# Reordering the second quad in the first batch: q turned before k, scores and exps by head pairs between AV units

## The chip, the cores and the metric

The kernel runs on one core of a Trainium2 chip. The metric is the device time of one execution in microseconds (us), median over several runs. Each ratio, with its 95% interval, is against runs of the kernel before. Kernels are compared only within the same rounds.

## The reference, cut to what matters

Eight batches of eight heads: attention of 512 local positions in a window of 32 to each side, plus 32 global positions that see and are seen by all. A gated feed-forward layer on the result (512 to 2048 to 512).

```python
k_all = np.concatenate([k_g, k_l], axis=2)
s_g   = scale * np.matmul(q_g, k_all.transpose(0, 1, 3, 2))      # global rows see everything
out_g = np.matmul(sm(s_g), v_all)
s_ll  = np.where(np.abs(pos[:, None] - pos[None, :]) <= 32, scale * q_l @ k_l.T, -1e9)
s_l   = np.concatenate([scale * q_l @ k_g.T, s_ll], axis=-1)
out_l = np.matmul(sm(s_l), np.concatenate([v_g, v_l], axis=2))
...
h = x @ w_in
return (h * sigmoid(1.702 * h)) @ w_out
```

## The kernel before: the parts concerned

Four heads make a quad; the first batch is quads `a` and `c`. A quad's scores come in two rounds, each a tile of four PSUM banks, one bank a head. `psS` holds one such tile; a ring of four one-bank tiles, `psP`, serves everything else (K's scores `kb`, the AV units `ov`, and so on).

```python
psS = ctx.enter_context(tc.tile_pool(name="psS", bufs=1, space=bass.MemoryType.PSUM))
psP = ctx.enter_context(tc.tile_pool(name="psP", bufs=4, space=bass.MemoryType.PSUM))
... # class Quad (cut)
    def B(self, rnd, split=False):        # the window's bias, added on TensorE: 8 matmuls of 128x128
    def S(self, rnd, ...):                # scores: 2 chunks x 2 halves of d, 4 heads in 4 row groups
        for c in (2 * rnd, 2 * rnd + 1):
            ...                           # rows and columns of the chunk (cut)
            for e in range(2):
                for j in range(4):
                    p = slice(32 * j, 32 * j + 32)
                    nc.tensor.matmul(ps[j][:, off : off + n], lhsT=self.k[p, 128 * c : 128 * c + 128, e],
                                     rhs=self.q[p, lo:hi, r0 : r0 + nr, e], ...)
    def X(self, rnd):                     # exps: all four banks in one ACTIVATE
        ...                               # the branch for scores in four separate tiles (cut)
        nc.scalar.activation(e[:, :, :RW], self.ps[:, :, :RW], AF.Exp, scale=scale)
        if rnd == self.gr:                # the global rows' exp
            nc.scalar.activation(e[:, 2, RW:], self.ps[:, 2, RW : RW + 32], AF.Exp, scale=scale)
```

`Tk` and `Tq` turn (transpose) k and q on VectorE, `ext` adds q's extra rows; `gg` and `K` are small 32x32 matmuls of the global part, `XK` is K's exp; `ekU(u)` and `U(u)` are the AV unit u, exps times values (0 is the softmax's sum, 1 and 2 the values); `R` and `XL` normalise, and `XL` writes what the first hidden matmuls read. The schedule of the first batch:

```python
a.X(1)
c.Tk(); c.ext(); c.Tq()
cast_g32("v", rvg)
c.B(0); a.K(); a.XK()
c.S(0, added=True); c.gg(); c.X(0)
a.eg(); c.K(); c.XK()
a.ekU(0); a.U(0); a.R()
a.ekU(1); a.U(1); a.XL(0)
c.B(1); c.S(1, added=True); c.X(1)
a.ekU(2); a.U(2); a.XL(1); a.Gm()
... # then c's three AV units, c.R, c.XL and the first hidden matmuls, which wait for c.XL
```

The softmax here doesn't subtract the row's maximum and nothing guards it: scores larger than these inputs give would overflow.

Of the kernel before, what the change touches and what calls it, by code (L numbers as in the profile page):

```python
# [15 lines left out]
AF = mybir.ActivationFunctionType  # L16
# [4 lines left out]
def kernel(  # L21
# [12 lines left out]
    nc = tc.nc  # L34

    B, H, Sl, D = q_l.shape
    Sg = q_g.shape[2]
    S = Sg + Sl
    n_tokens = B * S
    d_model = H * D  # L40
    d_ff = moe_w_in.shape[1]
    assert (B, H, Sl, Sg, D) == (8, 8, 512, 32, 64)
    W = 32
    scale = 1.0 / (D ** 0.5)
# [6 lines left out]
    RW = 428  # L51
# [62 lines left out]
    def cast_g32(name, t):  # L114
        nc.vector.tensor_copy(t[:, 0:2, :D], g32[name])
# [67 lines left out]
    def near(t, c):  # L183
        lo = 0 if c else 2
        return t[:, :, lo : lo + WIN[c][1]]
# [44 lines left out]
    def pbank(name):  # L230
        return psP.tile([128, 512], F32, name=name, tag="p")

    class Quad:
# [37 lines left out]
                    qgT[:, self.Q, : n * nr].rearrange("p (t r) -> p t r", t=n))  # L271


        def B(self, rnd, split=False):
            self.bk[rnd] = [pbank("s") for _ in range(4)] if split else self.spt(rnd)
            ps = self.bk[rnd] if split else [self.bk[rnd][:, j, :] for j in range(4)]
            for c in (2 * rnd, 2 * rnd + 1):
                w = (40, 200, 36, 228)[c]
                for j in range(4):
                    nc.tensor.matmul(ps[j][:, w : w + 16 * WIN[c][1]], lhsT=ident, rhs=near(bias, c),  # L280
                                     start=(c == 2 * rnd), stop=False, skip_group_check=True)

        def S(self, rnd, split=False, added=False, part=None):
            if not added:
                self.bk[rnd] = self.spt(rnd)
            ps = self.bk[rnd] if split else [self.bk[rnd][:, j, :] for j in range(4)]
            for c in (2 * rnd, 2 * rnd + 1):
                off = (0, 200, 0, 228)[c]
                r0, nr = WIN[c]
                t0, t1 = ((0, 20), (4, 23), (1, 20), (4, 24))[c]  # L290
                lo, hi = ((t0, t1) if part is None else (12, t1) if part else (t0, 12))
                off += (lo - t0) * nr
                n = (hi - lo) * nr
                for e in range(2):
                    for j in range(4):
                        p = slice(32 * j, 32 * j + 32)
                        nc.tensor.matmul(  # L297
                            ps[j][:, off : off + n],
                            lhsT=self.k[p, 128 * c : 128 * c + 128, e],
                            rhs=self.q[p, lo:hi, r0 : r0 + nr, e],  # L300
                            start=(e == 0 and not added), stop=(e == 1), skip_group_check=True,
                        )
            if not part:
                self.E[rnd] = att.tile([128, 4, RW + 32], BF16, name="e%d" % rnd)
            if split:
                self.gk(ps[2][:, RW : RW + 32], self.qg)
            self.ps = self.bk[rnd]
# [9 lines left out]
                                     rhs=rv[:, :, ee] if len(rv.shape) == 3 else rv[:, :, :, ee],  # L317
                                     start=(ee == 0), stop=(ee == 1), skip_group_check=True)

        def X(self, rnd):  # L320
            e = self.E[rnd]
            if isinstance(self.ps, list):
                for j in range(4):
                    n = RW + 32 if j == 2 else RW
                    nc.scalar.activation(e[:, j, :n], self.ps[j][:, :n], AF.Exp, scale=scale)
                return
            nc.scalar.activation(e[:, :, :RW], self.ps[:, :, :RW], AF.Exp, scale=scale)  # L327
            if rnd == self.gr:
                nc.scalar.activation(e[:, 2, RW:], self.ps[:, 2, RW : RW + 32], AF.Exp, scale=scale)

        def M(self, rnd):
            at = 36 if rnd else 40
            e = self.E[rnd][:, :, at : at + LW]
            nc.vector.tensor_mul(e, e, mask[:, rnd : rnd + 1, :].to_broadcast([128, 4, LW]))  # L334
# [161 lines left out]
    def o_out(i, tci, op):  # L496
        ob = moe.tile([128, d_model], F32, name="ob", bufs=6)
        last = i == B and tci == B // 4 - 1
        for lo, hi in ((0, 320), (320, 512)) if last else ((0, 512),):
            if last:  # L500
                op = pbank("op")
                for fc in range(FC):
                    nc.tensor.matmul(op[:, lo:hi], lhsT=gTs[i][:, fc, tci * 128 : tci * 128 + 128],  # L503
                                     rhs=w_out_sb[:, fc, lo:hi], start=(fc == 0), stop=(fc == FC - 1))
            nc.scalar.activation(ob[:, lo:hi], op[:, lo:hi], AF.Copy, scale=0.5)  # L505
            for j in range(4):
                eng = nc.scalar if last and j % 2 else nc.sync
                if i < B:
                    rows = out[i * S + Sg : (i + 1) * S, :].rearrange("(r t) m -> t r m", t=16)[4 * tci + j]
                else:  # L510
                    r = (4 * tci + j) * S
                    rows = out[r : r + Sg, :]
                eng.dma_start(out=rows[:, lo:hi], in_=ob[32 * j : 32 * j + 32, lo:hi])
# [8 lines left out]
    a, c = Quad(0), Quad(1)  # L522

    def zero(n, ps):
        for _ in range(n):
            nc.tensor.matmul(ps, lhsT=warm[:, 0:128], rhs=warm, start=False, stop=False, skip_group_check=True)
# [25 lines left out]
    a.S(1, split=True, added=True)  # L552
    zero(3, a.bk[1][3])
    a.X(1)
    c.Tk()
    c.ext()
    c.Tq()
    cast_g32("v", rvg)
    c.B(0)
    a.K()  # L560
    a.XK()
    c.S(0, added=True)
    c.gg()
    c.X(0)
    a.eg()
    c.K()
    c.XK()
    a.ekU(0)
    a.U(0)
    a.R()  # L570
    a.ekU(1)
    a.U(1)
    a.XL(0)
    c.B(1)
    c.S(1, added=True)
    c.X(1)
    a.ekU(2)
    a.U(2)
    a.XL(1)
# [42 lines left out]
    a, c = nq[1]  # L622
# [49 lines left out]
    a, c = nq[2]  # L672
# [83 lines left out]
    for i in range(1, B):  # L756
        if i > 1:
            for fc in range(FC):
                h_step(i, fc)
        if i + 1 < B:  # L760
            phase_o(i)
# [36 lines left out]
```

## Time and profile before

| | before |
|---|---|
| time, median of 3 runs | 311.05 us (310.76 to 311.09) |
| span of the profiled run | 309.3 us |
| TensorE / VectorE / ScalarE busy | 97% / 68% / 54% |
| first scores of `c` start | 12.20 us |
| AV of `c` starts | 18.05 us |
| first matmul that waits for `c.XL` | 21.19 us |

How to read it: TensorE is the bound, and from 21.19 us on it has hardly an idle moment. Up to there it waits on loads, turns and exps. So a change in this stretch is worth what it moves the moment at 21.19, if nothing behind takes it back. The lines are in the prediction.

### The profile page before, as it was taken

The page shows a single profiled execution, that of the slowest core. Times are in us where ns is not written, and L with a number is a line of the kernel's source. Part 1 is how long each engine was busy: PE and PEld are TensorE (multiplying, and loading weights), DVE is VectorE, ACT ScalarE, POOL GpSimd, SP SyncE. Part 2 cuts the span into 40 slices and gives each one's busy share as a digit, 9 for nine tenths or more (in the row PEclk, how much of TensorE's full clock was granted, in tenths as well). Part 3 has the DMA queues.
Part 4 walks back from the last instruction along what each step waited for, and adds up shares of the span by engine and source line. Part 5 has one row for each costly group of instructions (what it writes and reads, how often), then busy time and mean ns, then how long its engine had stood idle before and what let it go on. Part 6 is the DMA issues. An engine that isn't in the chain of part 4 may idle for free.

```text
span 309.3 us, 7765 instructions
## 1 busy us (share of the span) xinstructions
PE 299.2 (97%) x3230; PEld 149.3 (48%) x3265; DVE 211.0 (68%) x446; ACT 167.6 (54%) x251; POOL 54.1 (18%) x86
## 2 busy tenths in 40 slices
PE   7899999999999999999999999999999999999994
PEld 6544445444454455444454455445454454446653
DVE  6668857978957876776867876776777855573320
ACT  4728475475546735565556645565456651673421
POOL 8542754630050001400050002100000000000000
PEclk9999999999999999999999999999999999999999
DMA  7999999999289013951199013901120012201122
GB/s 193 176 209 206 201 138 217 213 184 100 61 79 192 5 36 72 131 107 30 45 95 173 8 37 71 101 0 36 36 61 10 2 44 46 51 0 35 35 68 69
DMA packets 53859, 27.60 MB, mean 89 GB/s; under 512 B 42432, under 2 KB 43712, under 8 KB 53824
## 3 DMA queue, kind: packets, MB, share of 16 engines
q0 software_dynamic: 45696, 16.95, 48.2%
q1 hardware_dynamic: 7648, 9.51, 12.6%
q10 hardware_dynamic: 480, 0.66, 0.7%
q8 instruction: 25, 0.41, 0.6%
q14 instruction: 10, 0.08, 0.1%
HBM read 35.13 MB, written 8.91 MB: 142 GB/s over the span
## 4 chain that ended last, share of the span: by engine, by line
PE 88%; DVE 4%; ACT 2%; DMA 2%; issue 1%; POOL 1%; ACTq 0%; POOLq 0%
PE op L491 35%; PE hp L466 35%; PE s L297 6%; PE ov L397 4%; PE ov L374 3%; DMA rk<-in_k_l_dram 2%; ACT e L327 1%; DVE xL L430 1%; PE s L316 1%; PE op L503 1%; DVE gT L474 1%; PE s L466 1%; PE s L415 1%; ACT th L473 1%; PE kb L316 1%
## 5 line engine op out<-in xcount | busy, mean ns | idle before, releaser
L491 PE MATMUL op<-w_out_sb,gT 128*128 128x512 bf16 x504 | 120.0, 380 | 1.7 <-issue 0.5
L474 DVE SCALAR_TENSOR_TENSOR gT<-th,hp 128x512 bf16<-128x512 f32 (+1 forms) x140 | 91.1, 656 | 41.8 <-ACT th L473 40.5
L466 PE MATMUL hp<-xL,w_in_sb 128*128 128x512 bf16 x487 | 108.4, 379 | 0.7
L473 ACT ACTIVATE th<-hp 128x512 f32<-128x512 f32 (+1 forms) x140 | 79.8, 573 | 42.9 <-PE hp L466 39.4
L466 PEld LDWEIGHTS <-w_in_sb 128*128 128x128 bf16 x576 | 56.1, 98 | 65.0 <-issue 1.3
L491 PEld LDWEIGHTS <-gT 128*128 128x128 bf16 x528 | 49.3, 98 | 56.4 <-issue 3.5
L327 ACT ACTIVATE e<-s 128x1712 bf16<-128x1712 f32 x31 | 49.5, 1597 | 15.8 <-PE s L415 8.9
L505 ACT ACTIVATE ob<-op 128x512 f32<-128x512 f32 (+2 forms) x35 | 20.5, 585 | 60.3 <-PE op L491 57.7
L89 POOL DMA_DIRECT2D v<-in_v_l_dram x24 | 18.7, 786 | 115.9 <-PE s L415 111.0
L421 DVE STREAM_TRANSPOSE sT<-ov 128x512 f32<-128x512 f32 x15 | 10.8, 717 | 29.1 <-PE ov L397 29.1
L334 DVE TENSOR_TENSOR e<-e,mask 128x1408 bf16<-128x1408 bf16 x28 | 24.4, 871 | 6.5 <-ACT e L327 6.5
L297 PE MATMUL s<-q,kT 32*128 32x228 bf16 (+5 forms) x528 | 21.1, 280 | 0.9 <-DVE q L259 0.7
L430 DVE TENSOR_TENSOR xL<-ov,rs 128x512 bf16<-128x512 f32 x30 | 19.4, 686 | 1.8 <-PE ov L397 0.5
L297 PEld LDWEIGHTS <-kT 32*128 32x128 bf16 x528 | 11.1, 95 | 14.8 <-issue 9.4
L255 DVE STREAM_TRANSPOSE kT<-rk 128x512 f32<-128x512 f32 (+1 forms) x17 | 16.9, 993 | 1.4 <-DMA rk<-in_k_l_dram 1.3
L362 ACT ACTIVATE ek<-kb 128x512 bf16<-128x512 f32 x16 | 9.6, 601 | 9.5 <-PE kb L316 9.5
L397 PE MATMUL ov<-e,v 128*32 128x160 bf16 (+1 forms) x480 | 12.1, 239 | 0.0
L425 DVE STREAM_TRANSPOSE rs<-rT 128x512 f32<-128x512 f32 x16 | 11.4, 711 | 0.5
L259 DVE STREAM_TRANSPOSE q<-rq 128x512 f32<-128x512 f32 (+1 forms) x17 | 10.7, 634 | 0.0
L397 PEld LDWEIGHTS <-v 128*32 128x32 bf16 x512 | 10.0, 97 | 0.9 <-issue 0.9
L316 PE MATMUL kb<-q,kgT 32*32 32x512 bf16 x128 | 10.0, 386 | 0.0
L466 PE MATMUL hp<-xG,w_in_sb 128*128 128x256 bf16 x64 | 9.6, 273 | 0.1
(78 smaller groups left out, 165.9 us busy)
## 6 DMA issues: line engine op xcount, KB each, us to landing
out_dram<-ob SPq DMA_DIRECT2D x132, 64.0 KB, 1.7
v<-in_v_l_dram POOLq DMA_DIRECT2D x32, 128.0 KB, 6.5
rq<-in_q_l_dram POOLq DMA_DIRECT2D x6, 512.0 KB, 8.5
rk<-in_k_l_dram POOLq DMA_DIRECT2D x6, 512.0 KB, 10.4
w_out_sb<-in_moe_w_out_dram POOLq DMA_DIRECT2D x4, 512.0 KB, 11.3
w_in_sb<-in_moe_w_in_dram POOLq DMA_DIRECT2D x4, 256.0 KB, 10.2
w_in_sb<-in_moe_w_in_dram POOLq DMA_DIRECT2D x2, 512.0 KB, 12.5
rq<-in_q_l_dram POOLq DMA_DIRECT2D x3, 256.0 KB, 7.9
```

Of the source, the lines that this page charges most:

```text
L89: nc.gpsimd.dma_start(out=vtiles[b % 2][p, s, :, :, :D], in_=vf[b, g][:, hs])
L255: nc.vector.transpose(self.kT.rearrange("p (r t) -> p t r", t=16)[:, lo:hi], loaded[self.b][0][:, self.u].bitcast(F32)[:, 32 * lo : 32 * hi])
L297: nc.tensor.matmul(ps[j][:, off : off + n], lhsT=self.k[p, 128 * c : 128 * c + 128, e], rhs=self.q[p, lo:hi, r0 : r0 + nr, e], start=(e == ...
L327: nc.scalar.activation(e[:, :, :RW], self.ps[:, :, :RW], AF.Exp, scale=scale)
L334: nc.vector.tensor_mul(e, e, mask[:, rnd : rnd + 1, :].to_broadcast([128, 4, LW]))
L397: nc.tensor.matmul(ov[32 * j : 32 * j + 32, :].rearrange("p (t r) -> p t r", t=16)[:, :, r0 : r0 + nr], lhsT=lv, rhs=self.E[c // 2][:, j, ...
L430: nc.vector.tensor_mul(self.x[:, 2 * self.u + h, :], self.st[1 + h], self.st["rs"])
L466: nc.tensor.matmul(hp[:, : width(i)], lhsT=w_in_c[:, fc // 8, kc, fc % 8 // 2, :, fc % 2], rhs=(xL[i] if i < B else xG)[:, kc, :], start=( ...
L473: nc.scalar.activation(th[:, :n], hp[:, :n], AF.Tanh, scale=0.851)
L474: nc.vector.scalar_tensor_tensor(gTs[i][:, fc, :n], in0=th[:, :n], scalar=1.0, in1=hp[:, :n], op0=ALU.add, op1=ALU.mult)
L491: nc.tensor.matmul(op, lhsT=gTs[i][:, fc, tci * 128 : tci * 128 + 128], rhs=w_out_sb[:, fc, :], start=(first and fc == 4 * f4), stop=(fc = ...
L505: nc.scalar.activation(ob[:, lo:hi], op[:, lo:hi], AF.Copy, scale=0.5)
```

## The change

The intent: q lands before k, so turn it in that idle time; do the scores and exps of `c` two heads at a time, so that the second scores of a pair can go into the banks that the first pair's exp has freed; and fill TensorE's waits with the AV units of `a`. The core of the diff:

```diff
-        def S(self, rnd, split=False, added=False, part=None):
+        def S(self, rnd, split=False, added=False, part=None, js=range(4)):
...
-                    for j in range(4):
+                    for j in js:
...
+            if js is not None:
+                nc.scalar.activation(e[:, js, :RW], self.ps[:, js, :RW], AF.Exp, scale=scale)
+                return
...
-    c.Tk()
+    c.Tq()
     c.ext()
-    c.Tq()
+    c.Tk()
...
-    c.X(0)
+    c.X(0, slice(0, 2))
+    c.X(0, slice(2, 4))
+    c.Xg()
     a.eg()
-    c.K()
-    c.XK()
     a.ekU(0)
     a.U(0)
     a.R()
+    c.K()
+    c.B(1, js=(0, 1))
+    c.S(1, added=True, js=(0, 1))
+    c.X(1, slice(0, 2))
+    c.XK()
     a.ekU(1)
     a.U(1)
     a.XL(0)
-    c.B(1)
-    c.S(1, added=True)
-    c.X(1)
+    c.B(1, js=(2, 3))
+    c.S(1, added=True, js=(2, 3))
+    c.X(1, slice(2, 4))
```

More of the change, by code (lines that the diff above doesn't have):

```diff
@@ L271, in ext, with B @@
                     qgT[:, self.Q, : n * nr].rearrange("p (t r) -> p t r", t=n))
-        def B(self, rnd, split=False):
-            self.bk[rnd] = [pbank("s") for _ in range(4)] if split else self.spt(rnd)
+        def B(self, rnd, split=False, js=range(4)):
+            self.bk[rnd] = [pbank("s") for _ in range(4)] if split else self.pt if len(js) < 4 else self.spt(rnd)
             ps = self.bk[rnd] if split else [self.bk[rnd][:, j, :] for j in range(4)]
@@ L294, in S @@
                 for e in range(2):
-                    for j in range(4):
+                    for j in js:
                         p = slice(32 * j, 32 * j + 32)
@@ L302, in S @@
                         )
-            if not part:
+            if not part and 0 in js:
                 self.E[rnd] = att.tile([128, 4, RW + 32], BF16, name="e%d" % rnd)
@@ L318, in gk, with X @@
                                      start=(ee == 0), stop=(ee == 1), skip_group_check=True)
-        def X(self, rnd):
+        def X(self, rnd, js=None):
             e = self.E[rnd]
+            if js is not None:
+                nc.scalar.activation(e[:, js, :RW], self.ps[:, js, :RW], AF.Exp, scale=scale)
+                return
             if isinstance(self.ps, list):
@@ L329, in X, with Xg @@
                 nc.scalar.activation(e[:, 2, RW:], self.ps[:, 2, RW : RW + 32], AF.Exp, scale=scale)
+        def Xg(self):
+            nc.scalar.activation(self.E[self.gr][:, 2, RW:], self.ps[:, 2, RW : RW + 32], AF.Exp, scale=scale)
         def M(self, rnd):
@@ L554 @@
     a.X(1)
+    c.Tq()
+    c.ext()
     c.Tk()
-    c.ext()
-    c.Tq()
     cast_g32("v", rvg)
```

## The prediction

> **What bounds the kernel now.** I read the page first, then the chain of waits over the first 50 us, then the timeline engine by engine from 8 to 24 us, down to windows of tens of ns.
>
> ```profile
> PE 299.2 (97%) x3230; PEld 149.3 (48%) x3265; DVE 211.0 (68%) x446; ACT 167.6 (54%) x251; POOL 54.1 (18%) x86
> ...
> PE 88%; DVE 4%; ACT 2%; DMA 2%; issue 1%; POOL 1%; ACTq 0%; POOLq 0%
> ```
>
> TensorE (PE) is busy for 97% of the span and is 88% of the chain that ended last: whatever moves PE's dense part earlier or later moves the end. The change touches only the first batch, before that dense part begins at 21.19 us (from 21.19 to 33.40 us PE is busy 12.16 of 12.21). So the question is when the matmul that starts at 21.19 us will start. The chain of waits up to it:
>
> ```profile
> 3.02 7.18 DMA rk<-in_k_l_dram
> ...
> 11.13 0.40 DVE q L269 x4
> 11.53 0.63 DVE q L259
> ...
> 12.20 0.67 PE s L297 x16
> ...
> 13.08 1.60 ACT e L327
> ...
> 14.81 0.77 PE s L280 x8
> ...
> 16.98 0.70 DVE xL L430
> ...
> 17.72 0.40 PE ov L374 x4
> 18.12 0.45 PE ov L397 x15
> ```
>
> The second quad's k lands at 10.20, is turned on VectorE (DVE), then come q's extra rows and q, then the scores (12.20), their exp (13.08), the second bias and scores (14.81), and then not those scores' exp but the first quad's last normalisation (16.98): the second quad's third AV bank is the buffer which that frees at 17.67. At 18.05 its AV units start, and its R, XL and the wait for them lead to 21.19, 3.14 us later. The timeline of PE and ScalarE (ACT):
>
> ```profile
> 12.85 0.39 PE L374 MATMUL ov<-ek,ones 32*32 32x512 bf16 x4
> 12.86 0.62 PE L316 MATMUL kb<-q,kgT 32*32 32x512 bf16 x8
> 13.41 0.49 PE L397 MATMUL ov<-e,ones 128*32 128x160 bf16 x16
> ...
> 12.02 0.64 ACT L362 ACTIVATE ek<-kb 128x512 bf16<-128x512 f32 x1
> 13.08 1.60 ACT L327 ACTIVATE e<-s 128x1712 bf16<-128x1712 f32 x1 [0.42 <-PE s L316]
> ...
> 16.23 1.60 ACT L327 ACTIVATE e<-s 128x1712 bf16<-128x1712 f32 x1 [0.98 <-PE s L297]
> ```
>
> From 12.70 to 18.05 PE is nearly full already (1.95 of 2.10 us, then 3.14 of 3.25): there is little idle time for a better order to fill.
>
> **What the Trainium skill says.** (1) "TensorE: Matmul & The Clock Gate", Part 3: matmuls in different row groups run concurrently, starting about 4 ns apart. The trace agrees: the four head matmuls of a scores step start within 12 ns (12.200 to 12.212) and the next step 105 to 133 ns later. So two heads need the same four steps as four heads. (2) "TensorEngine Tiling (Array Packing)", Key Properties: changing the tiling mode drains the array. The trace agrees: the last scores matmul starts at 12.576 and the next of another tile shape at 12.796; its 228 columns[...] are an estimated 95 ns, which leaves 125 ns; after K (last start 13.10, 213 ns of columns) U starts at 13.41, which leaves 97 ns. I take 0.1 us a change. (3) "ScalarE: Activation LUTs", What ACT_TABLE_LOAD costs: an ACTIVATE takes 186 ns and 0.833 ns an element, and neighbours overlap by some 93 ns. For 1712 elements that is 1612 ns, the trace has 1597; the two halves should start 0.78 us apart. (4) "PSUM — Partial Sum Buffer", PSUM bank collisions: guard PSUM by bank and quadrant. This program's own waits look coarser, by tile:
>
> ```profile
> 52.75 0.49 PE L397 MATMUL s<-e,ones 128*32 128x160 bf16 x16
> 53.07 0.78 PE L397 MATMUL s<-e,v 128*32 128x160 bf16 x32
> ...
> 53.90 0.72 DVE L421 STREAM_TRANSPOSE sT<-s 128x512 f32<-128x512 f32 x1 [0.33 <-PE s L397]
> ```
>
> The transpose reads only the bank of the first unit, whose matmuls end by 53.24, but it starts at 53.90, after the 53.85 end of the third unit, which is in another bank of the same four-bank tile. Also the tanh of banks 0 and 1 waits at 23.11 for the matmul into bank 3. In one-bank tiles units release one by one (sT starts at 18.59, while the other units still run).
>
> **The change part by part.**
>
> *q before k.* The second quad's q lands at 8.55, k at 10.20; DVE is idle from 8.91 to 10.22. Turning q (0.70) and its rows (0.40) fits in there, so the scores need only kT (10.22 + 1.05 = 11.27). But PE is then at the bias and K: K's last matmul starts at 11.46, with 0.21 and 0.10 of drain the array is free at 11.77. Scores start 11.77 instead of 12.20: 0.43 earned, not the 1.1 of DVE work. Of that AV gets less: gg ends issuing at 12.42, then ekU(0) needs ek, whose exp on ACT runs until 12.66 as before. ekU(0) starts at 12.71, U(0) at 13.03 (was 13.41).
>
> *K moved behind U(0).* Before, K and ekU(0) shared the array: both within 12.85 to 13.41, 0.56 us. Apart they take 0.32 (13.83 to 14.15 for another ekU) and about 0.56 (11.21 to 11.77): 0.31 more of PE. U(0) to K takes 0.42, so K 13.45, and PE is ready for the bias at 14.01.
>
> *Second scores by pairs.* Bias: 8 matmuls stay 8, 0.70 becomes 0.39 twice (one more drain). Scores: 0.60 from 15.51 to 16.11 for four steps; each pair needs four steps, so 0.56 twice: +0.52. All this on PE, in front of U(2).
>
> *The exps.* Only bank reuse can pay: the new bias goes into the banks of the first scores, no new tile. If waits go by bank it starts at 14.01. If by tile, as above, it must wait for the whole first exp: first half from 12.65, second 13.43, the global one 14.21 to 14.40, bias at 14.45, 0.44 later.
>
> **Sum, waits by tile.** Bias 14.45, scores 14.84, ekU(1) 15.40, U(1) 15.72; exp of pair one, 0.72 after its scores' start as at present, 15.56 to 16.46. PE is ready for the second bias at 16.14 but waits for that exp until 16.51. Scores 16.90, ekU(2) 17.46, U(2) 17.78. In the kernel before, U(2) starts at 16.43 and the second quad's AV at 18.05, 1.62 later, by XL(1) and the bank it frees; that stays, for exp of pair two ends at about 18.5 and does not bind. So AV starts at 19.40: **1.35 us late**.
>
> **Sum, waits by bank.** Bias 14.01, scores 14.41, ekU(1) 14.96, U(1) 15.28, bias 15.70, scores 16.10, ekU(2) 16.65, U(2) 16.97, AV 18.59: **0.54 us late**. In both, the second exp ends at 17.7 to 18.5, hardly before or even after the 17.83 of today, so the pairs earn nothing.
>
> Behind it all stays in order, and nothing absorbs the shift: the weights for the eighth hidden chunk land at 25.89 and are used at 27.2, the last output weights at 39.00 and are used at 41.3, and the third k at 41.87, used by scores at 47.06. A later start only widens these. So the delay goes through to the end, one for one.
>
> **Rivals.** (a) Faster by some 0.4 to 0.6 us: the scores' earlier start goes through. For it: 0.43 at 12.20, and the chain runs through q and the first exp. Against: PE is almost full from there on, and the change adds about 0.9 us of PE time in front of U(2) (0.31 + 0.08 + 0.52). It would need pairs at half the cost of four heads, U(2) at about 16.0: 310.5. (b) Waits by bank, only PE time added: 311.6. (c) Waits by tile, 312.4. (d) Hidden anyway: the second exp ended at 17.83, only 0.2 us before AV, and if the bank freed by XL(1) stopped binding, AV could start about when PE gets there: within 0.2 of 311.05. Against: the order of buffers at that point is unchanged, XL(1) still needs U(2). (e) A transfer becomes the bound: only if PE ran over 1.2 us early, which nothing here gives.
>
> **Range and chances.** I give (c) about 0.7, (b) 0.2, (a) and (d) 0.1. That puts the middle at 312.2. Runs of the kernel before differ by 0.3, another chip may add as much. Range 311.1 to 312.9. Two per cent is 6.2 us, over four times the largest shift here: a verdict of "same" is nearly sure.
>
> **What would show it.** The q transpose at about 8.8 to 9.5, and the first score of the second quad near 11.8, show step one. K alone for 0.56 after U(0) shows the lost sharing. Eight scores in about 0.56 rather than 0.30 show that pairs don't halve. The bias with a wait on the global exp (tile) or none (bank) tells (c) from (b). The first matmul that now waits for XL at 21.19 should be at about 22.5 (c) or 21.7 (b), and the rest of the trace displaced by as much. The prediction is wrong if pairs cost 0.3 each, if PE can run K beside U, or if the later part takes back the delay, to be seen if the shift at 21.19 is not the shift of the span.

## The result, and the profile after

The changed kernel took 311.45 us (median of 6, 311.14 to 311.94) against 310.99 for the kernel before (6 runs); the ratio is 1.0014, interval 1.0001 to 1.0027. A second set gave 311.71 against 310.90, ratio 1.0026 (1.0013 to 1.0040). A ratio is the mean time of one kernel's fast runs over that of the other's of the same rounds, so it is not quite the ratio of the medians. The verdict is "same" at 2%, with a small loss that both intervals hold clear of zero, the first barely: 0.14 to 0.26% of 311 us, 0.4 to 0.8 us.

First the page's lines of the engines and of the chain, in the changed kernel:

```profile
PE 299.6 (97%) x3230; PEld 149.1 (48%) x3265; DVE 211.3 (68%) x446; ACT 167.8 (54%) x253; POOL 54.1 (17%) x86
...
PE 90%; ACT 3%; DVE 3%; DMA 1%; issue 1%; ACTq 0%
```

As many matmuls as before and two ACTIVATEs more. The chain of waits (start, length, what; `issue` is time in which the engine waited for nothing that the profile shows) shows what changed:

```profile
1.28 4.37 DMA k<-in_k_l_dram
...
9.67 1.71 ACT e L328 x4
11.38 0.49 ACT ek L368
11.87 1.65 ACT e L323 x2
13.52 0.10 ACT e L335
13.62 0.04 issue
13.66 0.46 PE s L280 x4
14.12 0.61 PE s L297 x8
14.73 0.02 issue
14.75 0.89 ACT e L323
15.64 0.04 issue
15.69 0.46 PE s L280 x4
16.15 0.59 PE s L297 x8
```

Read it against the chain before. There the DMA at its head was the load of `c`'s k, then VectorE's turns. Here it is the load of `a`'s k, then `a`'s exps, K's exp, both halves of `c`'s first exp and the global one (13.52), and only then the bias of the first pair (13.66), its scores, its exp, and again only after that exp the bias of the other pair (15.69). The pairs go through strictly one after the other. TensorE's timeline has the two waits behind it, and what eight score matmuls cost (start, length, what; a bracket gives the engine's idle time just before and what ended it):

```profile
13.66 0.46 PE L280 MATMUL s<-bias,ident 128*128 128x192 bf16 x4 [0.36 <-ACT e L335]
14.05 0.66 PE L297 MATMUL s<-q,kT 32*128 32x228 bf16 x8
14.64 0.40 PE L380 MATMUL ov<-ek,rvg 32*32 32x512 bf16 x4
14.96 0.49 PE L403 MATMUL ov<-e,v 128*32 128x160 bf16 x16
15.69 0.46 PE L280 MATMUL s<-bias,ident 128*128 128x192 bf16 x4 [0.23 <-ACT e L323]
```

The bias of heads 0 and 1 waits for the global exp, which reads bank 2; the bias of heads 2 and 3 waits for an exp of banks 0 and 1. Neither uses the other's bank. And the eight scores occupy the array from 14.05 to 14.64, 0.59 us, where sixteen took 0.60 (15.51 to 16.11) in the kernel before:

```profile
15.51 0.67 PE L297 MATMUL s<-q,kT 32*128 32x228 bf16 x16
16.11 0.40 PE L374 MATMUL ov<-ek,rvg 32*32 32x512 bf16 x4
```

The moments of several traces, for all that follows. X is the start of `a`'s first exp, L the landing of `c`'s k, S the start of `c`'s first scores, AV that of its AV units.

| trace | X | L | S | AV | S to AV |
|---|---|---|---|---|---|
| before | 8.87 | 10.20 | 12.20 | 18.05 | 5.85 |
| changed | 8.08 | 9.80 | 10.98 | 18.61 | 7.63 |
| changed, second trace | 9.22 | 10.64 | 12.13 | 19.76 | 7.63 |
| changed, k first | 8.36 | 10.91 | 12.91 | 20.54 | 7.63 |
| changed, two tiles | 8.16 | 10.19 | 11.31 | 18.00 | 6.69 |
| q first, K late | 8.87 | 10.30 | 11.78 | 17.70 | 5.92 |
| q first alone | 8.27 | 10.01 | 11.17 | 17.02 | 5.85 |
| copies on ScalarE | 8.43 | 10.77 | 12.77 | 18.62 | 5.85 |

Clock times can't be compared across rows, since X and L differ by 1.1 us from run to run whatever the kernel; differences within a row can, and they repeat to 0.01 us. With k first, S is L + 2.00 in all three rows. With q first it is X + 2.91, or L + 1.1 to 1.2 where k is late.

### The profile page after: what moved, and what is told of

Same layout as the page of the kernel before. It is cut to its first block, busy times and chain, and to the rows that moved or that the text cites. A ratio compares the mean times of both kernels' runs of the same rounds, so it can differ in the third digit from the quotient of the medians.

```text
span 309.4 us, 7768 instructions
## 1 busy us (share of the span) xinstructions
PE 299.6 (97%) x3230; PEld 149.1 (48%) x3265; DVE 211.3 (68%) x446; ACT 167.8 (54%) x253; POOL 54.1 (17%) x86
## 4 chain that ended last, share of the span: by engine, by line
PE 90%; ACT 3%; DVE 3%; DMA 1%; issue 1%; ACTq 0%
PE op L497 37%; PE hp L472 36%; PE s L297 6%; PE ov L403 4%; PE ov L380 3%; DMA k<-in_k_l_dram 1%; ACT e L330 1%; DVE xL L436 1%; ACT e L323 1%; PE op L509 1%; PE s L316 1%; PE s L472 1%; PE s L421 1%; ACT e L328 1%; PE kb L316 1%
## 5 line engine op out<-in xcount | busy, mean ns | idle before, releaser
L330 ACT ACTIVATE e<-s 128x1712 bf16<-128x1712 f32 x29 | 46.3, 1597 | 14.0 <-PE s L421 8.9
```

## The experiments

Theory: q first earns, and the pairs lose, by two terms: matmul time (a pair costs what four heads cost) and waits that fall on the whole four-bank tile. Rivals: the pairs lose by matmul time alone; K's new place loses; q first is hidden.

**q first alone.** The only edit to the kernel before:

```diff
-    c.Tk()
+    c.Tq()
     c.ext()
-    c.Tq()
+    c.Tk()
```

> Kernel before with only the first part of the change: the second quad's q turned ahead of its k. Theory (q first earns, the rest of the change loses): from the first quad's first exp to the first matmul that waits for the second quad's XL it took 12.32 us before (8.87 to 21.19) and 13.67 in the changed kernel (8.08 to 21.75); here it takes 11.9, and the time is 310.4 to 310.7, 0.1 to 0.2% below before. Rival (q first is hidden, because the array is held by the first quad's K anyway): 12.3 and 311.0.

Measured: 310.03 us against 310.94, ratio 0.9985 (0.9962 to 1.0007; one run of six at 312.28 widens it). The stretch from X took about 11.96 us: the first hidden matmuls waited for a load of weights and then ran until 20.23, worked out as 18.715 plus seven spacings of 0.216, since one record is missing.

> q first alone once more, beside the version above: its first time was 310.03 with an interval that reached no difference. Theory: 310.0 to 310.4 and a ratio of 0.997 to 0.999; the first scores to AV take 5.85 us as before and start 1.1 to 1.2 us after k lands or 2.9 us after the first quad's exp starts, whichever is later. Rival: no difference from before, 310.9.

Measured: 310.00 against 310.95, ratio 0.9991 (0.9959 to 1.0023; one run of six at 313.51). S to AV was 5.84, S came 2.91 after X. The medians are 0.9 us below before both times, but these two intervals reach no difference; what secures the gain is the trace (S no longer 2.00 after L) and the comparisons below with k first again, K late and the last version.

**The changed kernel with k first again.** The same edit undone:

> The changed kernel with k turned first again. Theory: the order of the turns is a gain of 0.4 us or more inside a net loss, so the stretch takes 14.0 to 14.3 us and the time is 311.8 to 312.2. Rival (the turns do nothing): 13.7 and 311.45.

Measured: 312.38 us, ratio 1.0046 (1.0033 to 1.0059). So the turns' order is a gain inside the net loss. The direction met the theory; both figures went beyond it, the time by 0.2 us and the stretch, 15.32 us, by a whole one, because in that trace k landed late (10.91), and with k first all waits for that. S to AV is 7.63 as in the changed kernel, so the loss sits entirely behind S.

**q first and K late**, scores and exps whole and in their old places:

```diff
     a.eg()
-    c.K()
-    c.XK()
     a.ekU(0)
     a.U(0)
     a.R()
+    c.K()
+    c.XK()
```

> q first, and K and its exp moved behind the first quad's U(0) and R; scores and exps whole and in their old places. Theory: K apart costs PE 0.3 to 0.4 us which nothing hides: the stretch takes 12.2 to 12.3 us, the time about 310.9. Rival (only the pairs lose): as q_first, 11.9 and 310.6.

Measured: 310.39 us, ratio 0.998 (0.9968 to 0.9992), stretch 11.97, S to AV 5.92: 0.07 us more than q first alone, not the 0.3 expected. The timeline of TensorE shows why:

```profile
13.46 0.41 PE L316 MATMUL kb<-q,kgT 32*32 32x512 bf16 x4
13.49 0.40 PE L374 MATMUL ov<-ek,rvg 32*32 32x512 bf16 x4
13.71 0.40 PE L316 MATMUL kb<-q,kgT 32*32 32x512 bf16 x4
14.03 0.49 PE L397 MATMUL ov<-e,v 128*32 128x160 bf16 x16
14.46 0.78 PE L280 MATMUL s<-bias,ident 128*128 128x192 bf16 x8
```

K was not apart: it now shared the array with the next unit's `ekU(1)`, as it had with `ekU(0)`. `ekU(1)` to U(1) takes 0.57 us instead of 0.32, so K adds 0.25. And of that 0.18 fills a wait: with q first alone the bias came 0.60 us after U(1)'s start, held by the global exp, here 0.43. So this run does not test K alone on the array, as it was meant to. From 5.92 to the changed kernel's 7.63, 1.71 us, is what the pairs and a K that stands alone do together.

**Pairs in two tiles of two banks.** The changed kernel, with `c`'s scores in two tiles instead of one, so that a wait by tile is a wait by pair:

```diff
+    class Two:
+        def __init__(self, pool):
+            self.t = [pool.tile([128, 2, 512], F32, name="s2%s" % h) for h in "ab"]
...  # an index of head j goes to tile j // 2, bank j % 2
     cast_g32("v", rvg)
+    psA.__exit__(None, None, None)
+    psB = pool4("psB")
+    c.pt = Two(psB.__enter__())
     c.B(0)
...  # and back to one four-bank tile after a.Gm()
```

> The changed kernel, the second quad's scores in two tiles of two banks, so that a wait by tile is one by pair. Theory (of 1.35 us lost, some 0.8 are waits of the pair's bias on exps of the other pair, which fall on the same tile): the first bias no longer waits for the global exp and the second not for the first pair's new exp; the stretch takes 12.8 to 13.0 us and the time is 310.9 to 311.2. Rival (the loss is PE time alone: eight scores take as long as sixteen): 13.6 and 311.45.

Measured: 310.73 us, ratio 0.9992 (0.9980 to 1.0004), a little under the time expected; stretch 12.97, S to AV 6.69. TensorE's timeline of that run, the same matmuls as above:

```profile
12.75 0.63 PE L331 MATMUL kb<-q,kgT 32*32 32x512 bf16 x8
13.31 0.48 PE L295 MATMUL s2a<-bias,ident 128*128 128x192 bf16 x4
13.72 0.66 PE L312 MATMUL s2a<-q,kT 32*128 32x228 bf16 x8
14.31 0.40 PE L395 MATMUL ov<-ek,rvg 32*32 32x512 bf16 x4
14.64 0.49 PE L418 MATMUL ov<-e,v 128*32 128x160 bf16 x16
15.06 0.48 PE L295 MATMUL s2b<-bias,ident 128*128 128x192 bf16 x4
15.47 0.66 PE L312 MATMUL s2b<-q,kT 32*128 32x228 bf16 x8
```

Both waits are gone; the bias follows at once (no bracket). The eight scores still take 0.59 us (13.72 to 14.31). So of the 1.71 us, 0.94 (7.63 less 6.69) went with the waits by tile and 0.77 (6.69 less 5.92) remain. Against K late they add up from the two timelines: bias and scores take 1.00 us twice (13.31 to 14.31, 15.06 to 16.06) instead of 1.30 once (14.46 to 15.76), 0.70 more; K, alone here, takes 0.56 instead of 0.25, 0.31 more; and from S to `ekU(0)`, which waits for the exp of `a`'s K, it took 0.70 instead of 0.94, S being the later one in this trace. The rival of matmul time alone falls. And even with both exps free the pairs lose to whole scores: 6.69 against 5.85.

**The changed kernel again**, for a second trace:

> The changed kernel once more, for its time beside the same runs of before and a second trace. Theory (the steps of the prediction hold, and the first loads differ from run to run): the first scores of the second quad to its AV take 7.6 us again (7.63 in the first trace, 5.85 before), whatever the loads do; the time is 311.2 to 311.7. Rival (the first trace was a chance): 5.9 to 7.0.

Measured: 311.71 us, S to AV 7.63, the same two waits of 0.36 and 0.23. The steps repeat.

**Holding the first quad back.** Why then only 0.4 to 0.8 us, when 1.35 was worked out from the trace of before? Theory: before, the chain ran through k's landing and `a` had slack, so `a`'s late start in that trace (X at 8.87) cost nothing; the changed kernel has no such slack. Two matmuls of zeros put the halves of `a`'s first scores 0.90 us apart (7.55 to 8.45) instead of 0.32 (8.07 to 8.39):

```diff
     a.S(0, added=True, part=0)
+    zero(2, a.bk[1][3])
     a.S(0, added=True, part=1)
```

> Kernel before with two matmuls of zeros between the halves of the first quad's first scores, which hold the first quad's first exp back by 0.5 to 0.7 us. Theory (before, the second quad waits for its k and the DVE turns behind it, so a late first quad costs little): 0.0 to 0.2 us more, 311.0 to 311.2. Rival (the first quad's path binds before too): 0.5 to 0.7 us more.

> The changed kernel with the same two matmuls of zeros. Theory (after the change the chain runs through the first quad's exps): 0.5 to 0.7 us more than the changed kernel, 312.0 to 312.2. Rival (the first quad has slack here too): 0.0 to 0.2 us more.

Measured: before, held: 310.86 us, ratio 0.9998 (0.9986 to 1.0011), nothing. Changed, held: 311.96, ratio 1.0039 (1.0027 to 1.0052), against 1.0026 unheld in the same rounds: 0.13%, about 0.4 us more. The first met the theory, the second fell short of the 0.5 to 0.7 expected, and its interval overlaps the unheld one. Nor does its one trace show the hold at work: there the chain ran through the late load of `a`'s global k (landed at 9.09) and the matmuls behind it, and S, at 11.74, came 3.10 us after X (8.64) where the step of `a`'s path is 2.91. So this pair of runs does not show the theory; what carries it is the table, where S is X + 2.91 in both traces of the changed kernel and L + 2.00 in that of before.

**Small copies on ScalarE.** In the trace of before the second batch's scores came 17.12 us after the first matmul that waits for XL; in both traces of the changed kernel 16.88. The last three lines of VectorE ahead of those scores, and GpSimd's at the same time, in the kernel before:

```profile
37.44 0.19 DVE L200 STREAM_TRANSPOSE qgT<-rqg 128x64 f32<-128x64 f32 x1
37.56 0.20 DVE L200 STREAM_TRANSPOSE kgT<-rkg 128x64 f32<-128x64 f32 x1
37.69 0.59 DVE L269 COPY q<-qgT 128x40 f32<-128x40 f32 x4
...
35.82 1.66 POOL L206 DMA_DIRECT2D v<-in_v_l_dram  x2
37.42 0.81 POOL L101 DMA_DIRECT2D rkg<-in_k_g_dram  x1
```

and in the changed kernel:

```profile
38.25 0.45 DVE L269 COPY q<-qgT 128x40 f32<-128x40 f32 x4
```

The four copies overlap in the records. In windows of tens of ns they last 0.16 to 0.18 us each in the changed kernel; in the kernel before the four last 0.56, 0.49, 0.39 and 0.31 and end between 38.25 and 38.27, just as GpSimd's issue of a load does (37.42 + 0.81 = 38.23). The transposes beside it kept their length. "SBUF — State Buffer", Who interferes with whom, says that a VectorE copy in a two-port mode and GpSimd exclude each other for a whole instruction, and that ScalarE never waits for them. The ends here agree with it, and so they do in three more traces (before held, q first alone, and one copy of K late), within 0.04 us. But an overlap alone does not hold a copy: in the changed kernel's second trace GpSimd issued from 39.24 to 39.92, and the copies from 39.41 on took 0.16 to 0.23. And no view shows in which mode a copy ran. So that the copies were held is shown; that the ports did it is argued. The edit, on the kernel before:

```diff
-    a.ext()
+    a.ext(act=True)          # nc.scalar.copy instead of nc.vector.tensor_copy, second batch only
```

> Kernel before with the second batch's four small copies of q's extra rows on ScalarE instead of VectorE. Theory (in the trace of before those copies ended together when GpSimd's issue of a load ended, 0.31 to 0.56 us each instead of 0.17, and the scores behind them came 0.24 us later after the first matmul that waits for XL than in the changed kernel: 17.12 against 16.88): here it is 16.88 to 16.95 and the time 310.7 to 310.9. Rival (that 0.24 us has another source): 17.1.

Measured: the distance was 16.88, as expected, so the 0.24 us were these copies. The time was 311.10, ratio 1.0004 (0.9991 to 1.0018), above the 310.7 to 310.9 expected: the gain is not to be seen in it. In that trace k landed late, at 10.77; whether that hid it is not shown. The copies were held in both traces of before (with the held one: 17.12 and 17.09) and in none of the three of the changed kernel (16.88 each). That is luck of timing: of the two traces of q first alone, one has 17.13 and one 16.88. It takes some 0.24 us of the loss back.

**A version that beats both.** q first alone had one new wait, in its TensorE timeline:

```profile
18.71 3.41 PE L466 MATMUL s<-xL,w_in_sb 128*128 128x512 bf16 x15 [0.60 <-DMA w_in_sb<-in_moe_w_in_dram]
```

The load it waited for landed at 18.67 and brings other columns of the weights than these matmuls read; only the matmuls of the second contraction chunk wait for it. So the first chunk goes first for all four columns, and the second batch's copies go to ScalarE:

```diff
-    for fc in range(4):
-        h_mm(0, fc, pt[:, fc, :], (0, 1))
+    for kc in (0, 1):
+        for fc in range(4):
+            h_mm(0, fc, pt[:, fc, :], (kc,))
...
-    a.ext()
+    a.ext(act=True)
```

> q first alone, with two small things that its trace asked for: the first hidden matmuls in the order of the contraction chunks (there the second of them sat 0.60 us waiting for a load of input weights), and the second batch's extra rows copied on ScalarE. Theory: the wait shrinks below 0.2 us and the stretch from the first matmul after XL to the second batch's scores is 16.9 us; the time is 309.7 to 310.1, 0.3 us below q first alone. Rival (the load wait only moves to the next chunk): as q first, 310.0 to 310.4.

```profile
18.46 1.90 PE L466 MATMUL s<-xL,w_in_sb 128*128 128x512 bf16 x8
20.57 1.89 PE L466 MATMUL s<-xL,w_in_sb 128*128 128x512 bf16 x8 [0.21 <-DVE xL L430]
```

Measured: there is no wait for the load, the distance to the second batch's scores is 16.88, and the time is 309.76 us against 310.95, ratio 0.9963 (0.9951 to 0.9976): 1.2 us better than before, and the best of all. But in this trace the load landed at 18.30, before the first hidden matmul at 18.46, so the old order would not have waited either: what the new order is worth is not shown. The time is 0.24 us below q first alone of the same submission (310.00), within that one's interval, and these runs do not part the two additions.

## Why the prediction was right or wrong

- *The bound.* Right for the first batch. The matmul behind XL decides, and from AV to it took 3.14 us in the traces of before and of the changed kernel alike.
- *Waits by tile.* Right, rival (c) as it was called. From S at 11.77 to AV at 19.40 the prediction had 7.63 us; three traces have 7.63. It had 0.44 and 0.37 us for the two waits, from when the array was ready; counted so the trace has 0.44 (13.22 to 13.66) and 0.31 (15.38 to 15.69). The brackets' 0.36 and 0.23 count from the modelled ends of the matmuls.
- *Waits by bank.* 6.82 (18.59 less 11.77) predicted, 6.69 measured in two tiles: right within 0.13, and in part by luck, since S to `ekU(0)` took 0.70 there and not 0.94. From `ekU(0)` on it was 5.88 predicted, 5.99 measured.
- *Pairs don't halve.* Right: 0.59 us for eight scores, 0.56 predicted. The 95 ns for 228 columns, behind the 0.1 us for a change of tile shape, agree with the trace: matmuls of 512 columns follow each other every 0.216 us, which makes 96 ns for 228.
- *The halves of the exp.* 186 ns, 0.833 an element and an overlap of 93 make 0.81 us from one half to the next, not the 0.78 written; the trace has 0.78 (11.86 to 12.64), so nothing came of the slip.
- *K apart.* Right: 0.31 us more where K stands alone and nothing waits (two tiles). In the changed kernel itself it lies inside the wait for the global exp: K is through by 13.22 (12.66 + 0.56), the bias starts at 13.66.
- *q first, 0.43 us.* The term that was mis-sized. The step itself held: K late, with X at 8.87 as in the trace of before, has S at 11.78, `ekU(0)` at 12.72 and U(0) at 13.04, where the prediction had 11.77, 12.71 and 13.03. But it was worked out on a trace in which `a` was late against k. There L + 2.00 is 12.20 and X + 2.91 is 11.78: 0.42 earned. In the changed kernel's own trace L + 2.00 would be 11.80 and S was 10.98: 0.82 earned. From X and L of ten traces (all but the two held ones), AV of the changed kernel would be 0.93 to 1.36 us later than before's, 1.08 on average. That is an estimate: the later of X + 2.91 and L + 1.15, plus 7.63, less L + 2.00 + 5.85.
- *"Nothing absorbs the shift."* Wrong, and by the prediction's own sign: the matmul behind XL came 0.56 us later (21.19 to 21.75), the end of the span 0.15 (309.28 to 309.43). Of the difference 0.24 us are the held copies, and 0.17 lie behind the last matmul: from there to the end it is 4.02 us before and 3.85 in the changed kernel. ScalarE's queue (ACTq) paused longer between two of its last output transfers, first before, then changed:

```profile
304.45 0.38 ACTq L513
304.83 0.32 issue
305.15 0.34 ACTq L513
...
304.77 0.38 ACTq L519
305.15 0.04 issue
305.19 0.43 ACTq L519
```

  All five traces with as many ScalarE instructions as before (251) have the pause of 0.32, all seven with more have 0.04; why is not shown.

Together (1.08 less 0.17, less 0.24 where before's copies are held) that makes an estimated 0.7 to 0.9 us, where 1.35 was the sum and 0.4 and 0.8 were measured. The intervals of the two sets reach from 0.03 to 0.84 and from 0.40 to 1.24; 0.7, for held copies as in both traces of before, lies in both, so nothing clear of noise is left over. The range, 311.1 to 312.9, held the result; the middle, 312.2, was 0.5 to 0.75 too high.

## What to carry to other kernels

Work put side by side on row groups is not divided by splitting it: two heads hold the array as long as four, so split only where the first half's result is needed early. Before planning to reuse part of a tile, look in the trace whether waits come by the part or by the whole tile. And when a chain starts with loads, read the slack of every branch from more than one trace: a branch that was late for free in one kernel sets the pace in the next.

## What the Trainium skill lacked or had wrong

- "PSUM — Partial Sum Buffer", PSUM bank collisions: the rule by bank (and quadrant) is no guide to what a compiled program waits for. Here waits fell on the four-bank tile: 0.36 and 0.23 us of idle time, for exps of banks that the waiting matmuls do not touch, gone with two tiles (S to AV 7.63 to 6.69 us). I found no page that says so.
- "TensorEngine Tiling (Array Packing)", Key Properties, gives no figure for the drain at a change of mode: an estimated 0.10 to 0.13 us here, from starts of matmuls and their columns.
- "TensorE: Matmul & The Clock Gate", Part 3, states the gain of packing; that half the row groups take as long as all of them follows from its span model but is not said: 0.59 us for eight matmuls, 0.60 for sixteen.
- "SBUF — State Buffer", Who interferes with whom, has whoever issues first block the other for the whole instruction, where the copy is in a two-port mode. Here GpSimd's issue of a load came first both where the copies were held to its end (0.31 to 0.56 us) and where they ran on in 0.16 to 0.23; spans on GpSimd are rough, and what tells the two apart is not shown.
- None of the pages I read has the spread of first loads: over the twelve traces here the 256 KB load of `c`'s k landed between 9.80 and 10.91 us and `a`'s first exp started between 8.08 and 9.22.
